# Linear attention and a two-layer Mish network: the hand-written order replaced by a list scheduler, both layers by seven products, attention by whole chunks

## The chip, the cores and the metric

The kernel runs on one core of a Trainium2 chip. The time is the device time of one execution in microseconds, taken as the median of several runs. A core has five engines that run side by side, each working through its own queue in order: TensorE (PE, matrix products), VectorE (DVE), ScalarE (ACT), GpSimd (POOL) and SyncE (SP, which issues transfers). They wait for one another by semaphores.

## The reference

The inputs are q, k, v of shape (4, 8, 768, 64) in fp32: 4 batches, 8 heads, 768 positions, 64 channels; `lam`, one decay for each head; w_in (512 x 2048) and w_out (2048 x 512).

```
for each block b of positions:
    intra = (qb kb^T * Dmask) vb                  # Dmask[i,j] = lam^(i-j) for i >= j, else 0
    inter = (qb * lam_pow) kv_state               # what earlier blocks left
    out[b] = intra + inter
    kv_state = lam_block * kv_state + (kb * rev_pow)^T vb
x = out, heads side by side                       # 3072 tokens x 512
h = x @ w_in
y = (h * tanh(softplus(h))) @ w_out               # Mish between the layers; 3072 x 512, fp32
```

## The kernel before

Both kernels take chunks of 128 positions. A **group** is one chunk of each of the four batches, 512 tokens; there are six groups, n = 0 to 5. For a group the attention makes `xt` (channels on the partitions, 4 x 512, fp16), the first layer makes h transposed in pieces of 128 x 512, Mish on ACT writes them to `hsg` in fp16, and the second layer multiplies `hsg` with `wout`.

**Attention** is done by half chunks, four heads each (`att_a`, `att_s`, `att_o`). From group 2 on, DVE scales q (`qT`, line 318) and copies k into `kz` (line 322), a tile in which the other head's 64 channels are zero, so that scores (`pS`, line 358) are products over all 128 partitions. DVE masks the scores into `sb` (line 362). `pO` (lines 375 and 379) adds up state and chunk; ACT copies it into `xt` (line 382). `pv` (line 283) is the new part of the state, which DVE adds (`raw`, line 298) and POOL multiplies with the decay (`w`, line 299). q and k arrive in fp16: POOL's queue casts them on the way. POOL scales k (`ktil`, line 259), and transfers that transpose, issued by SP, turn both (`qraw`, `kraw`, line 268); groups 0 and 1 are turned by PE.

**The first layer** is plain: 16 pieces of four products with 512 columns (`ph`, line 420). **The second layer** is plain in group 0 (`po`, line 442). From group 1 on it is done by seven products in place of eight (Strassen's way in Winograd's form; `fast_unit`, line 525): tokens, inner dimension and columns are halved, sums of quarters of `hsg` (`gsum`, line 498) and of `wout` (`tsum`, line 479) are made on DVE, and the seven products of 16 matmuls with 256 columns are gathered in `x`, `y`, `z`. ACT and DVE bring them out (`p1`, `p7`, `u3`, `osum`), POOL makes one difference (line 578).

**The order** is written out by hand. Each group has a list of `units`, the first layer's 16 pieces and then the second layer's 14; attention pieces of the next group are dealt out between them by `room`. An engine's queue is what this order leaves for it, and PSUM tiles have fixed uses by tag. The last group's last product lies in three PSUM tiles, `fin`, so that the last store is small.

**Loads** of q, k, v (but the first q and k) and of both weights go through POOL's queue, in the order chunks 0 to 3, `win` in six pieces, `wout` in four, chunk 4 and on. At most eight of its transfers are open: one waits until the eighth before it has landed.

Of the kernel before, what the change touches and what calls it, by code (L numbers as in the profile page):

```python
# [7 lines left out]
F32 = mybir.dt.float32  # L8
# [5 lines left out]
def bc(ap, axis, n):  # L14
    shape = list(ap.shape)
    shape.insert(axis, n)
    return ap.unsqueeze(axis).broadcast_to(shape)


@with_exitstack  # L20
def kernel(
# [19 lines left out]
    GT = B * C  # L41
    MID = C // 2 - 1
    NVB = 8
    NKB = 4
    NT = 2
# [3 lines left out]
    loads = ctx.enter_context(tc.tile_pool(name="loads", bufs=NVB))  # L49
    work = ctx.enter_context(tc.tile_pool(name="work", bufs=2))  # L50
    ps = ctx.enter_context(tc.tile_pool(name="ps", bufs=1, space=bass.MemoryType.PSUM))


    kn = [None] * (NG * B)
    qn = [None] * (NG * B)

    vz = [const.tile([128, H, 2 * D], F16, name=f"vz{i}") for i in range(NVB)]

    def chunk_rows(t, i):
        n, b = divmod(i, B)  # L60
        return t[b, :, n * C : (n + 1) * C, :].rearrange("h p c -> p h c")

    def load_k(i):
        if i == 0:
            kn[i] = const.tile([128, H, D], F32, name="kn0")
            nc.sync.dma_start(out=kn[i], in_=chunk_rows(k, i))
            return
        kn[i] = loads.tile([128, H, D], F16, name="kn", tag="kn")
        nc.gpsimd.dma_start(out=kn[i], in_=chunk_rows(k, i))  # L69

    def load_q(i):
        if i == 0:
            qn[i] = const.tile([128, H, D], F32, name="qn0")
            nc.scalar.dma_start(out=qn[i], in_=chunk_rows(q, i))
            return
        qn[i] = loads.tile([128, H, D], F16, name="qn", tag="qn")
        nc.gpsimd.dma_start(out=qn[i], in_=chunk_rows(q, i))  # L77

    def load_v(i):
        nc.gpsimd.dma_start(out=vz[i % NVB][:, :, 0:D], in_=chunk_rows(v, i))  # L80

    WS = 4

    cuts = (0, 128, 256, DF // WS)
    win0 = [const.tile([128, NKC, b_ - a_], F16, name=f"win0{a_}") for a_, b_ in zip(cuts, cuts[1:])]
    win = [None] + [const.tile([128, NKC, DF // WS], F16, name=f"win{s}") for s in range(1, WS)]
    wout = [const.tile([128, NKI // WS, DMO], F16, name=f"wout{s}") for s in range(WS)]

    def load_win(s):
        w = DF // WS  # L90
        if s == 0:
# [661 lines left out]
```

## Time and profile before

| | |
|---|---|
| runs | 219.47, 221.75, 222.33 us; median 221.75 |
| the profiled execution | span 217.4 us, from the first instruction to the last; the page has no other time of it |
| around the span | 4.35 us from the span to the median |
| busy in the span | PE 204.8, DVE 146.1, POOL 116.6, ACT 101.3 us |
| granted TensorE clock | 1.000 over the whole span |
| first product on the second piece of `win` | 21.13 us |
| last product | 214.06 us |

A row of the profile's groups names the line, the engine, the operation, out<-in, how often, the busy time and the mean of one in ns. A mean is the time from start to end of one instruction; two in a row on an engine overlap, so they follow each other at less than that. The chain of waits goes back from the last instruction, at each step to what released it.

### The profile page before, as it was taken

The numbers are of one execution on the slowest core, as the hardware profiler recorded it, in microseconds if no ns is written. First come the engines' busy times: TensorE is split into PE (matmuls) and PEld (weight loads), VectorE is DVE, ScalarE is ACT, GpSimd is POOL, SyncE is SP. The second block draws the span as 40 slices with busy tenths as digits, with TensorE's granted clock in tenths as the row PEclk, the third lists the DMA queues.
The fourth block names the chain that finished last, engine by engine and source line by source line (L and its number), as shares of the span: only waits on it lengthen the run. The fifth ranks groups of instructions, "written<-read, shape, count | busy, mean of one in ns | idle before, by whom it ended". The sixth has DMA issues, their size and how long they took to land.

```text
span 217.4 us, 4272 instructions
## 1 busy us (share of the span) xinstructions
PE 204.8 (94%) x1672; PEld 136.6 (63%) x1672; DVE 146.1 (67%) x309; ACT 101.3 (47%) x190; POOL 116.6 (54%) x139
## 2 busy tenths in 40 slices
PE   7899999999999799999979999979999999999993
PEld 2465544576545587745669845669845699644893
DVE  6667561877669999339999419999439987213433
ACT  5465566567665231166522176623166632266410
POOL 7996334998988768808757908757700002000020
PEclk9999999999999999999999999999999999999999
DMA  9999999999999999975999965999985201300014
GB/s 133 141 158 198 203 203 175 175 152 125 150 149 104 100 75 121 163 152 70 104 71 113 142 160 74 119 75 71 151 168 100 48 3 48 130 18 0 0 59 137
DMA packets 103766, 24.66 MB, mean 113 GB/s; under 512 B 93890, under 2 KB 103234, under 8 KB 103746
## 3 DMA queue, kind: packets, MB, share of 16 engines
q0 software_dynamic: 78080, 13.37, 80.3%
q1 hardware_dynamic: 22688, 8.39, 17.8%
q10 hardware_dynamic: 2978, 2.62, 4.0%
q8 instruction: 13, 0.21, 0.4%
q14 instruction: 7, 0.06, 0.1%
HBM read 27.26 MB, written 6.29 MB: 154 GB/s over the span
## 4 chain that ended last, share of the span: by engine, by line
PE 63%; DVE 20%; POOL 5%; issue 4%; DMA 4%; ACT 1%; ACTq 0%; POOLq 0%; DVEq 0%
PE ph L420 26%; PE z L525 10%; PE po L442 6%; PE y L525 6%; PE x L525 5%; DVE qT L318 5%; DVE kz L322 4%; DVE sb L362 4%; DVE gsum L498 4%; DMA win<-in_moe_w_in_dram 4%; PE pO L379 3%; DVE raw L298 3%; PE pS L358 2%; PE fin L525 2%; POOL vz L80 2%
## 5 line engine op out<-in xcount | busy, mean ns | idle before, releaser
L420 PE MATMUL ph<-xt,win 128*128 128x512 f16 (+2 forms) x404 | 89.6, 368 | 0.5 <-ACT hsg L434 0.2
L434 ACT ACTIVATE hsg<-ph 128x512 f16<-128x512 f32 x96 | 57.0, 597 | 45.6 <-PE ph L420 45.5
L420 PEld LDWEIGHTS <-win 128*128 128x128 f16 x404 | 37.0, 98 | 35.1 <-issue 0.6
L299 POOL TENSOR_TENSOR w<-raw,lbm 128x256 f16<-128x256 f32 x32 | 25.2, 791 | 29.0 <-DVE raw L298 28.9
L578 POOL TENSOR_TENSOR u<-u,p 128x512 f32<-128x512 f32 x5 | 6.5, 1293 | 52.0 <-DVE u L576 52.0
L525 PEld LDWEIGHTS <-gsum 128*128 128x128 f16 x336 | 30.8, 98 | 3.5 <-issue 0.5
L362 DVE TENSOR_TENSOR sb<-pS,maskT 128x512 f16<-128x512 f32 x40 | 27.2, 683 | 2.0 <-PE pS L358 1.9
L382 ACT ACTIVATE xt<-pO 128x256 f16<-128x256 f32 x40 | 15.2, 382 | 27.4 <-PE pO L379 27.2
L318 DVE TENSOR_TENSOR qT<-qraw,lq 128x256 f16<-128x256 f16 x32 | 19.1, 598 | 10.3 <-DMA qraw<-qn 10.3
L525 PEld LDWEIGHTS <-hsg 128*128 128x128 f16 x240 | 22.7, 98 | 2.5
L69 POOL DMA_DIRECT2D kn<-in_k_dram x23 | 21.4, 932 | 4.5 <-DMA win<-in_moe_w_in_dram 1.7
L80 POOL DMA_DIRECT2D vz<-in_v_dram x24 | 21.7, 906 | 3.3 <-DMA wout<-in_moe_w_out_dram 1.7
L77 POOL DMA_DIRECT2D qn<-in_q_dram x23 | 20.7, 898 | 5.1 <-DMA wout<-in_moe_w_out_dram 3.3
L498 DVE TENSOR_TENSOR gsum<-hsg 128x1024 f16<-128x1024 f16 x20 | 14.5, 725 | 12.9 <-ACT hsg L434 12.9
L322 DVE COPY kz<-kraw 64x256 f16<-64x256 f16 x64 | 19.9, 311 | 1.9 <-DMA kraw<-ktil 0.9
L379 PE MATMUL pO<-sb,vz 128*128 128x128 f16 x160 | 17.3, 219 | 3.6 <-DVE sb L362 3.2
L525 PE MATMUL z<-tsum,gsum 128*128 128x256 f16 x160 | 20.4, 272 | 0.2
L525 PE MATMUL x<-wout,hsg 128*128 128x256 f16 x160 | 20.1, 273 | 0.0
L358 PE MATMUL pS<-qT,kz 128*128 128x128 f16 x160 | 16.6, 220 | 1.8 <-DVE kz L322 1.6
L358 PEld LDWEIGHTS <-kz 128*128 128x128 f16 x160 | 11.8, 98 | 7.8 <-DVE kz L322 3.0
L298 DVE TENSOR_TENSOR raw<-pv,w 128x256 f32<-128x256 f32 x32 | 13.5, 422 | 4.1 <-PE pv L283 3.4
L379 PEld LDWEIGHTS <-vz 128*128 128x128 f16 x160 | 12.6, 98 | 5.7 <-issue 4.9
(89 smaller groups left out, 242.8 us busy)
## 6 DMA issues: line engine op xcount, KB each, us to landing
out_dram<-osum SPq DMA_DIRECT2D x14, 256.0 KB, 3.2
vz<-in_v_dram POOLq DMA_DIRECT2D x24, 128.0 KB, 4.7
kn<-in_k_dram POOLq DMA_DIRECT2D x23, 128.0 KB, 4.4
qn<-in_q_dram POOLq DMA_DIRECT2D x23, 128.0 KB, 4.6
wout<-in_moe_w_out_dram POOLq DMA_DIRECT2D x4, 512.0 KB, 16.5
win<-in_moe_w_in_dram POOLq DMA_DIRECT2D x3, 512.0 KB, 10.1
out_dram<-osum ACTq DMA_DIRECT2D x5, 256.0 KB, 4.0
out_dram<-osb ACTq DMA_DIRECT2D x4, 256.0 KB, 5.5
```

The costliest lines, as they stand in the source:

```text
L69: nc.gpsimd.dma_start(out=kn[i], in_=chunk_rows(k, i))
L80: nc.gpsimd.dma_start(out=vz[i % NVB][:, :, 0:D], in_=chunk_rows(v, i))
L299: nc.gpsimd.tensor_tensor(out=w_new, in0=raw, in1=lb, op=ALU.mult)
L318: nc.vector.tensor_tensor(out=s.qT, in0=qraw[i][:, 2 * hf : 2 * hf + 2, :], in1=lqh, op=ALU.mult)
L322: nc.vector.tensor_copy(s.kz[rs, :, hp, :], kraw[i][rs, 2 * hf : 2 * hf + 2, :])
L358: nc.tensor.matmul(psS[:, 2 * p + hp, :], s.kz[:, p, hp, :], s.qT[:, p, :], start=True, stop=True,)
L362: nc.vector.tensor_tensor(out=s.sb, in0=psS, in1=bc(maskT, 1, 4), op=ALU.mult)
L379: nc.tensor.matmul(psO[:, p, :], vf[:, o : o + 128], s.sb[:, 2 * p + hp, :], start=False, stop=(hp == 1))
L420: nc.tensor.matmul(ph_t[ni][:, lo:hi], win0[min(ni, 2)][:, kc, max(ni - 2, 0) * 128 : max(ni - 2, 0) * 128 + 128] if ni < w else win[ni // ...
L434: nc.scalar.activation(hsg[n][:, ni, :], ph_t.pop(ni), AF.Mish)
L498: nc.vector.tensor_tensor(out=gsum[n, i][:, ks, :], in0=a, in1=b, op=op)
L525: nc.tensor.matmul(t, lhs(kk, b), rhs(kk, c, c + w), start=(fresh and kk == 0 and (alone or i == 0)), stop=(kk == HK - 1), skip_group_chec ...
```

## The change

The kernel is rewritten. The parts that matter:

- **Order.** `Plan.op` records every operation with its engine, an estimate of its duration, a rank, and what it reads and writes. `Plan.run` takes, step by step, the operation that can start first (among those within `SLACK` of it the one of lowest rank), picks its engine and its buffer (eight PSUM banks shared by everything, with a least number kept for each use), and the instructions are issued in the order of the starts that it reckons. The chip's engines still wait by semaphores alone.
- **First layer** of groups 1 to 5 by seven products of four matmuls with 256 columns for each quarter `s` of the inner dimension (`first_layer`). Sums that were made outside PSUM in the second layer are made here by copying one PSUM bank into another, in which the next product is then accumulated: three copies on ACT or DVE and two additions on DVE for each quarter. Sums of `xt` and of `win` are made on DVE.
- **Second layer** of all groups by seven products, group 0 too; a 256 KB store at the end of each of its four results, the last one too.
- **Attention** by whole chunks: scores are products over 64 partitions, the two heads of a pair on the two halves of the array, into two banks; no `kz`. POOL scales both q and k (in groups 0 and 1 DVE does most of it). k, q of groups 1 to 5 are loaded in fp32 by SP; group 1 is turned by PE, later ones by transfers as before.
- **Loads.** `win` in four pieces. A small ACT copy that reads `win[2]` stands ahead of group 1's k and q, a small POOL copy that reads the fourth of them ahead of `wout`.
- `lq` is a decay for each position and head, made once; two table loads on ACT go.
- Empty products (`zero`) fill PE's idle time up to the 45th microsecond that `Plan.run` reckons.

The diff, cut to its core (the tile allocations, the launch and the set-up of decays are left out; lines of the old kernel are those on attention, first layer and order that are named above):

```diff
-            nc.vector.tensor_tensor(
-                out=s.qT, in0=qraw[i][:, 2 * hf : 2 * hf + 2, :], in1=lqh, op=ALU.mult)
-            for hp in range(2):
-                rs = slice(64 * hp, 64 * hp + 64)
-                nc.vector.tensor_copy(s.kz[rs, :, hp, :], kraw[i][rs, 2 * hf : 2 * hf + 2, :])
...
-        psS = ps.tile([128, 4, C], F32, name="pS", tag=("pS", "pk")[s.seq % 2 if s.n >= NT else 0])
-        for p in range(2):
-            for hp in range(2):
-                nc.tensor.matmul(
-                    psS[:, 2 * p + hp, :], s.kz[:, p, hp, :], s.qT[:, p, :], start=True, stop=True,
-                )
...
-        if hsg[n] is None:
-            hsg[n] = work.tile([128, NKI, GT], F16, name="hsg", tag="hsg", bufs=2)
-        if ni in ph_t:
-            mm1_part(n, ni, GT - C, GT)
-        else:
-            mm1_part(n, ni, 0, GT)
-        nc.scalar.activation(hsg[n][:, ni, :], ph_t.pop(ni), AF.Mish)
...
-    for n in range(NG):
-        units = [(mm1_unit, (n, ni)) for ni in range(NKI)]
-
-        if n == 0:
-            units += [(mm2_unit, (n, b2 + b, part)) for b2 in range(0, B, 2) for part in range(WS)
-                      for b in range(2)]
-        else:
-            units += [(fast_unit, (n, step, blk)) for step in range(7) for blk in range(2)]
...
+TAIL = {PE: 0.20, ACT: 0.15, DVE: 0.14, POOL: 0.12, SP: 0.0}
+SLACK = {PE: 0.12, ACT: 0.12, DVE: 0.12, POOL: 0.2, SP: 0.2}
...
+        while ready:
+            best = {}
+            for o in ready:
+                at = max([o.after] + [d.start for d in o.behind])
...
+                    for e, took in o.ways.items():
+                        if o.svc is not None and len(asked.get(e, ())) >= 8:
+                            at = max(at, asked[e][-8])
+                        t = max([at, free[e]] + [d.end if d.eng == e == PE else d.seen for d in o.deps])
+                        best.setdefault(e, []).append((t, o, took))
...
+            e, t0 = min(((e, min(c[0] for c in cs)) for e, cs in best.items()), key=lambda x: x[1])
+            t, o, took = min((c for c in best[e] if c[0] <= t0 + SLACK[e]), key=lambda c: (c[1].rank, c[0]))
+            other = [(c[0] + c[2], x) for x, cs in best.items() for c in cs if c[1] is o and x != e]
+            if other and min(other)[0] < t + took:
+                e = min(other)[1]
+                t, o, took = next(c for c in best[e] if c[1] is o)
...
+    banks = Pool([psum.tile([128, 512], F32, name=f"bank{i}") for i in range(8)],
+                 {"l1": 4, "l2": 1, "at": 2})
+    full = Pool(tiles("full", 13, [128, 512], F32), {"es": 2, "raw": 1, "l2": 8})
+    given = Pool(tiles("given", 8, [128, 512], F32))
+    half = Pool(tiles("half", 11, [128, 512], F16), {"kt": 2, "qt": 1})
+    turns = Pool(tiles("turn", 8, [128, 512], F16))
...
+            if (n, b) == (0, 0):
+                qe, chain = (SP if x == "k" else ACT), None
+            else:
+                qe, chain = (POOL, "sw") if n < 1 else (SP, "hw")
+            op({qe: 0.87 if qe == POOL else 0.42}, lambda e, buf=buf, src=src: ENG[e].dma_start(
+                out=by_head(buf.t), in_=rows(src, n, b)), rank, writes=[buf], svc=0.87, after=after,
+               chain=chain)
...
+    def scaled(n, b, src, by, name, rank, ways):
+        t = Buf(half, "kt" if name == "lk" else "qt")
+        op(ways, lambda e: ENG[e].tensor_tensor(
+            out=by_head(t.t), in0=by_head(src.t), in1=bc(by, 2, D), op=ALU.mult), rank,
+           reads=[src, name], writes=[t], chain=name)
+        return t
...
+    def turned(src, rank):
+        t = Buf(turns)
+        op({SP: 1.24}, lambda e: nc.sync.dma_start_transpose(out=by_pair(t.t), in_=src.t), rank,
+           reads=[src], writes=[t], svc=0.6, chain="turn")
+        return t
...
+            qT = turn(qt, rank - 2)
+        pS = [Buf(banks, "at") for _ in range(2)]
+
+        def scores(e):
+            for j in range(JP):
+                for t in range(2):
+                    rs = slice(64 * t, 64 * t + 64)
+                    nc.tensor.matmul(by_pair(pS[t].t)[:, j, :], by_pair(kT.t)[rs, j, :], by_pair(qT.t)[rs, j, :],
+                                     start=(j == 0), stop=(j == JP - 1), skip_group_check=True)
...
+            op({POOL: 1.25}, lambda e: nc.gpsimd.tensor_tensor(
+                out=wst[b], in0=by_pair(raw.t), in1=lbm, op=ALU.mult), late,
+               reads=[raw, "lbm"], writes=[("state", b)])
...
+    def first_layer(n, s, xs, rank):
+        kh, k0 = s // 2, 4 * (s % 2)
+        if s % 2 == 0:
+            gq[n, kh] = Buf(gblk)
+        A, Bb, Cc, E = (Buf(banks, "l1"), Buf(banks, "l1", seeded=True), Buf(banks, "l1", seeded=True),
+                        Buf(banks, "l1"))
+        es = Buf(full, "es")
...
+        def mish(src, r, f2, key):
+            op({ACT: 0.49}, lambda e: nc.scalar.activation(
+                gq[n, kh].t[:, r, k0 + 2 * f2 : k0 + 2 * f2 + 2, :], two(src.t), AF.Mish), rank + key,
+               reads=[src, "table"], writes=[(gq[n, kh], r, s % 2, f2)])
+
+        prod(A, w(0, 0), x(0, 0), True, lo + [("win", s)], 0)
+        op(cp(512), lambda e: copy(e, Bb.t, A.t), rank, reads=[A], writes=[Bb])
+        prod(E, w(0, 1), xsum(0), True, [xs[0], ("ws1", s)], 0.1)
+        prod(A, w(1, 0), x(1, 0), False, lo + [("win", s)], 0.3)
+        prod(Bb, ws(0), xsum(1), False, [xs[1], ("ws2", s)], 0.2)
+        op(cp(512), lambda e: copy(e, es.t, E.t), rank + 0.2, reads=[E], writes=[es])
+        opened["l1"] = op(cp(512), lambda e: copy(e, Cc.t, Bb.t), rank + 0.1, reads=[Bb], writes=[Cc])
+        op({DVE: 0.60}, lambda e: nc.vector.tensor_tensor(out=Bb.t, in0=Bb.t, in1=es.t, op=ALU.add), rank + 0.3,
+           reads=[es], writes=[Bb])
+        prod(Cc, ws(1), xsum(2), False, [xs[2], ("ws3", s)], 0.2)
+        prod(Bb, ws(2), x(1, 1), False, hi + [("ws4", s)], 0.5)
+        op({DVE: 0.60}, lambda e: nc.vector.tensor_tensor(out=es.t, in0=Cc.t, in1=es.t, op=ALU.add), rank + 0.3,
+           reads=[Cc], writes=[es])
+        prod(Cc, w(1, 1), xsum(3), False, [xs[3], ("win", s)], 0.4)
+        mish(A, 0, 0, 0.8)
+        mish(Bb, 1, 0, 0.8)
+        mish(es, 1, 1, 0.8)
+        mish(Cc, 0, 1, 0.8)
...
+        def store(r, c, t, rk):
+            op({SP: 0.42}, lambda e: nc.sync.dma_start(
+                out=out_v[n * C : (n + 1) * C, 2 * r : 2 * r + 2, c * HN : (c + 1) * HN], in_=two(t.t)),
+               rank + rk, reads=[t], svc=0.8)
...
+    k_first = buffers(1, 0)[0]
+    op({ACT: 0.2}, lambda e: nc.scalar.activation(k_first.t[:, 0:1], win[2][:, 0, 0:1], AF.Copy), -595,
+       reads=[("win", 2)], writes=[k_first])
+    for b in range(B):
+        load(1, b, "kq", -590 + b)
+    k_late = buffers(1, 1)[1]
+    op({POOL: 0.1}, lambda e: nc.gpsimd.tensor_copy(wout[0][:, 0, 0:1], k_late.t[:, 0:1]), -581,
+       reads=[k_late], writes=[("wout", 0)], chain="sw")
+    for s in (0, 2, 1, 3):
+        load_wout(s, -580 + s)
...
+    for s in range(WS):
+        first_plain(0, s, 10 * s)
...
+    order = plan.run()
+    rest = {a: (gap, s) for a, gap, s in plan.idle(banks, 45.0, 0.4)}
+    for o in order:
+        o.fn(o.eng)
+        if o in rest:
+            for _ in range(int((rest[o][0] - 0.15) / 0.219)):
+                nc.tensor.matmul(rest[o][1].tile, zero[:, 0:128], zero, start=False, stop=True,
+                                 skip_group_check=True)
...
```

Three places in which the order is new. First **POOL's queue after the first chunks' loads** (each row issues a load). Before:

```order
L96 DMA win_81<-in_moe_w_in_dram 128x4x512
L96 DMA win_82<-in_moe_w_in_dram 128x4x512
L103 DMA wout_83<-in_moe_w_out_dram 128x4x512
L103 DMA wout_84<-in_moe_w_out_dram 128x4x512
L103 DMA wout_85<-in_moe_w_out_dram 128x4x512
L103 DMA wout_86<-in_moe_w_out_dram 128x4x512
L140 IOTA ei 128x128
L69 DMA kn<-in_k_dram 128x8x64
L77 DMA qn<-in_q_dram 128x8x64
```

and now, with `given_89` the q of chunk 5:

```order
L351 DMA win_161<-in_moe_w_in_dram 128x4x512
L351 DMA win_162<-in_moe_w_in_dram 128x4x512
L411 DMA vz_136<-in_v_dram 128x8x64
L411 DMA vz_137<-in_v_dram 128x8x64
L411 DMA vz_138<-in_v_dram 128x8x64
L411 DMA vz_139<-in_v_dram 128x8x64
L735 CAST wout_167<-given_89 128x1
L356 DMA wout_167<-in_moe_w_out_dram 128x4x512
L356 DMA wout_169<-in_moe_w_out_dram 128x4x512
```

`wout` has moved from right behind `win` to behind group 1's v and the fourth of group 1's k and q.

Second **DVE's queue at the second layer of group 0**: the sums of `wout` (`wos`, and one half of `wout` in place) and of the group's hidden values (`g`, `gsum`). Now:

```order
L364 TENSOR_TENSOR g_115<-g_115,g_116 128x1024
L364 TENSOR_TENSOR wos_172<-wout_170,wout_168 128x1024
L364 TENSOR_TENSOR wos_171<-wout_169,wout_167 128x1024
L364 TENSOR_TENSOR wout_168<-wout_168 128x4x256
L364 TENSOR_TENSOR wos_171<-wout_169,wos_171 128x1024
L364 TENSOR_TENSOR wos_172<-wout_170,wout_168 128x1024
L364 TENSOR_TENSOR g_115<-g_115,g_116 128x1024
L364 TENSOR_TENSOR wos_172<-wout_170,wos_172 128x1024
L364 TENSOR_TENSOR gsum_120<-g_115 128x1024 x2
L364 TENSOR_TENSOR gsum_121<-g_116,gsum_120 128x1024 x2
```

From the second row on all of them are behind the last piece of `wout` (`wout_170`). Before, the same eight sums (`tsum`) stood among the units of groups 0 and 1 and were first needed in group 1.

Third **ACT's queue in the first layer of a later group** (`hsg` before, `g` now: Mish; `bank` PSUM; `full` SBUF in fp32). Before:

```order
L434 ACTIVATE hsg<-ph 128x512 x11
L382 ACTIVATE xt<-pO 128x2x128
L434 ACTIVATE hsg<-ph 128x512 x3
L382 ACTIVATE xt<-pO 128x2x128
L434 ACTIVATE hsg<-ph 128x512 x2
```

and now:

```order
L252 ACTIVATE bank_70<-bank_65 128x512
L252 ACTIVATE full_75<-bank_67 128x512
L252 ACTIVATE full_76<-bank_66 128x512
L581 ACTIVATE g_115<-bank_65 128x512
L252 ACTIVATE bank_69<-bank_64 128x512
L252 ACTIVATE full_78<-bank_63 128x512
L581 ACTIVATE g_115<-full_75 128x512
L252 ACTIVATE bank_67<-bank_69 128x512
L581 ACTIVATE g_115<-bank_70 128x512
L581 ACTIVATE g_115<-bank_68 128x512
L581 ACTIVATE g_115<-bank_64 128x512
L252 ACTIVATE bank_63<-bank_66 128x512
```

Copies from bank to bank, for which PE's next product waits, now stand between the Mish instructions.

1041 lines of the change are left out of this document (501 added, 540 removed).

## The prediction

> **What bounds the kernel now.** I read the page's busy times first, then the busy time by stage, then the chain of waits, and last the rows of the groups and of POOL's queue that price single steps.
>
> ```profile
> PE 204.8 (94%) x1672; PEld 136.6 (63%) x1672; DVE 146.1 (67%) x309; ACT 101.3 (47%) x190; POOL 116.6 (54%) x139
> PE 63%; DVE 20%; POOL 5%; issue 4%; DMA 4%; ACT 1%; ACTq 0%; POOLq 0%; DVEq 0%
> ```
>
> PE is busy 94% of the span and it holds 63% of the chain; DVE holds 20%. Where DVE's 20% lies, the stages tell (start and end, length, then busy time of each engine). I cut them at the beginning of each group's first layer, as the chain shows it; the first cut is the product that waits for the second piece of `win`, the last one the end of PE.
>
> ```profile
> core 0: us, PE busy (x) PEld busy (x) DVE busy (x) ACT busy (x) POOL busy (x), PEclk, DMA share, GB/s
> 0.00:21.10 21.10, 17.80 (x144) 9.98 (x144) 14.29 (x38) 11.42 (x20) 18.08 (x28) 1.00 1.58 156
> 21.10:57.00 35.90, 35.42 (x276) 20.68 (x277) 23.34 (x52) 22.71 (x46) 24.73 (x30) 1.00 1.49 172
> 57.00:90.65 33.65, 31.01 (x261) 21.68 (x261) 26.41 (x52) 13.22 (x26) 27.98 (x32) 1.00 1.49 115
> 90.65:124.05 33.40, 31.98 (x274) 22.65 (x272) 25.52 (x52) 14.21 (x27) 22.20 (x26) 1.00 1.05 112
> 124.05:157.50 33.45, 32.02 (x273) 22.65 (x272) 25.54 (x52) 14.21 (x27) 21.10 (x24) 1.00 1.04 111
> 157.50:188.00 30.50, 30.50 (x257) 21.67 (x256) 21.49 (x48) 14.17 (x27) 1.27 (x1) 1.00 0.36 76
> 188.00:214.10 26.10, 26.04 (x192) 17.32 (x190) 9.27 (x17) 11.35 (x19) 1.27 (x1) 1.00 0.12 41
> ```
>
> Groups 4 and 5 (157.5 to 214.1) are PE without a gap, and the granted clock is 1.00 in every stage. In groups 1 to 3 DVE is busy 25.5 of 33.4 us, and the chain runs over it. To see what PE alone needs I take the pace of its products from pieces of the chain, and the pace of products over 64 partitions from the timeline.
>
> ```profile
> 187.97 13.81 PE ph L420 x64
> 201.78 1.75 PE x L525 x16
> 114.07 0.22 PE pS L358 x4
> 113.91 0.39 PE L358 MATMUL pS<-qT,kz 128*128 128x128 f16 x4
> 15.45 0.40 PE L230 MATMUL pS<-pqT,pkT 64*128 64x128 f16 x8
> ```
>
> A product of 512 columns follows the last after 13.81/64 = 0.216 us, one of 256 after 0.109, one of 128 after 0.055. In the last two rows eight products over 64 partitions take from start to end what four over 128 take: they run in pairs, so eight cost 0.22.
>
> So PE needs in a middle group before: first layer 13.8; second layer 7 x 16 x 0.109 = 12.2; attention 4 chunks x (8 scores + 12 outputs + 4 states) x 0.055 = 5.3; together 31.3. Groups 2 and 3 take 33.4: 2.1 are waits, DVE's.
>
> **The change part by part.**
>
> *PE's work.* First layer by seven products: 7 x 4 x 4 = 112 matmuls at 0.109 = 12.2 for 13.8, 1.6 less in each of groups 1 to 5. Scores in pairs: 4 x 0.22 = 0.9 less in each of groups 1 to 4's attention work. A middle group needs 12.2 + 12.2 + 4.4 = 28.9; group 4, without states, 28.0; group 5 24.5.
>
> *The hand-offs of the first layer.* They are new on the path: for each quarter a copy of a bank before the next product can begin, twice in a row, and an addition. In groups and timeline before, the nearest rows:
>
> ```profile
> L434 ACT ACTIVATE hsg<-ph 128x512 f16<-128x512 f32 x96 | 57.0, 597 | 45.6 <-PE ph L420 45.5
> 56.36 1.08 ACT L434 ACTIVATE hsg<-ph 128x512 f16<-128x512 f32 x2 [0.49 <-PE ph L420]
> L362 DVE TENSOR_TENSOR sb<-pS,maskT 128x512 f16<-128x512 f32 x40 | 27.2, 683 | 2.0 <-PE pS L358 1.9
> 13.24 1.29 DVE L234 TENSOR_TENSOR sb<-pS,dm 128x512 f16<-128x512 f32 x2 [0.49 <-PE pS L230]
> ```
>
> ACT takes 0.597 for one, but two follow each other after 1.08 - 0.597 = 0.49; DVE after 1.29 - 0.683 = 0.60. By the order ACT has 32 such instructions in a middle group (16 Mish, 9 copies in the first layer, 3 in the second, 4 of `xt`): 15.7 us of 29. DVE has 39: 35 at 0.60 and 4 sums of `xt` of half that size, 22.2 us. Neither is the bound over a group. Inside the first layer it is close: 25 on ACT make 12.3 us against PE's 12.2, though PE's last product of the layer waits for only 18 of them, 8.8 us. That a copy writes PSUM is in no row. It reads 512 columns of PSUM like these rows, which excludes less than ACT's 0.49; above I bound it by DVE's 0.683 with no overlap, and take 0.49, its nearest form. A hand-off is longer than that: four products at a pace of 0.055 take 0.39 from start to end (row above), so a result is out 0.17 after PE could go on; with ACT's whole 0.597 and two semaphores it is 0.84. A quarter's chain is five products of 0.44 and four hand-offs, 5.6 us; the order has two quarters in flight, which fits into 12.2 with a little to spare. I allow 1.2 us of waits in groups 1 to 3, 1.0 in groups 4 and 5, where there were 2.1 and none; bounds 0 and 3.5.
>
> *Transfers of q and k, scaling on POOL.* Per group POOL has 8 scalings, 4 states and one difference:
>
> ```profile
> L578 POOL TENSOR_TENSOR u<-u,p 128x512 f32<-128x512 f32 x5 | 6.5, 1293 | 52.0 <-DVE u L576 52.0
> L80 POOL DMA_DIRECT2D vz<-in_v_dram x24 | 21.7, 906 | 3.3 <-DMA wout<-in_moe_w_out_dram 1.7
> 91.93 1.22 SPq L268 DMA_TRANSPOSE qraw<-qn  x1
> 0.74 0.45 SPq L66 DMA_DIRECT2D kn<-in_k_dram  x1
> qraw<-qn SPq DMA_TRANSPOSE x16, 3.4
> ```
>
> 13 x 1.29 + 4 x 0.91 = 20.4 of 29 us. SP has 8 transposing issues of 1.22, 8 loads and 4 stores of 0.45, 15 us. Both run a group ahead, under the 12.2 us of a second layer; where that cover is gone, the first late transpose costs its landing, 3.4 us. I put them at nothing.
>
> *The start, and group 0.* POOL's queue shows when the weights land: each load waits until the eighth before it has landed.
>
> ```profile
> 18.72 0.92 POOL L69 DMA_DIRECT2D kn<-in_k_dram  x1 [0.42 <-issue]
> 21.39 0.87 POOL L77 DMA_DIRECT2D qn<-in_q_dram  x1 [1.75 <-DMA win<-in_moe_w_in_dram]
> 23.87 0.87 POOL L80 DMA_DIRECT2D vz<-in_v_dram  x1 [1.61 <-DMA win<-in_moe_w_in_dram]
> 26.42 0.88 POOL L69 DMA_DIRECT2D kn<-in_k_dram  x1 [1.67 <-DMA win<-in_moe_w_in_dram]
> ...
> 36.60 0.87 POOL L77 DMA_DIRECT2D qn<-in_q_dram  x1 [1.68 <-DMA wout<-in_moe_w_out_dram]
> ```
>
> The first quarter of `win` is in by 18.7, all of it by 26.4 and `wout` by 36.6, a piece each 2.55 us; q, k, v follow at POOL's 0.87. Now 4 loads of v and 8 of fp32 k, q come between: 26.4 + 12 x 0.87 + 4 x 2.55 = 47.0 for the last of `wout`. For SP's fp32 loads the trace has one of the kind, 3.0 us from issue to landing:
>
> ```profile
> kn<-in_k_dram SPq DMA_DIRECT2D x1, 256.0 KB, 3.0
> L498 DVE TENSOR_TENSOR gsum<-hsg 128x1024 f16<-128x1024 f16 x20 | 14.5, 725 | 12.9 <-ACT hsg L434 12.9
> ```
>
> Bounds for one of many are 0.64, a quarter of a weight piece (1 MB of fp32 in 2.55), and 1.5, half of the 3.0: 44.3 to 52 for `wout`. I keep 0.87, between them, the pace at which POOL fed such loads. PE by then has done its other work: first layer from about 18.7, 13.8 + turning 1.8 + states 0.9 + attention 4.4 + two early products 0.9 brings it to 40.5, and it idles for `wout`. Behind the last piece DVE makes nine sums before the product that needs the last of them, 9 x 0.69 (a little under the row's mean of 0.725, since they follow each other) = 6.2, and half of the second layer, 6.1, is still to come: group 0 ends at 59.3, say 59.0, for 57.0 before. So the gain of a seven-product layer there (1.6) and of the pairs is lost in the wait for `wout`: +2.0 (bounds -0.5 and +8).
>
> *The end.* The last result is one addition and one 256 KB store, where there were small pieces:
>
> ```profile
> 214.08 0.29 DVE osum L562
> out_dram<-osum SPq DMA_DIRECT2D x14, 256.0 KB, 3.2
> out_dram<-osum SPq DMA_DIRECT2D x2, 64.0 KB, 1.7
> ```
>
> Addition 0.68 for 0.29, landing up to 3.2 for 1.7, shorter in an empty queue: 4.6 from PE's end to the span's for 3.3, +1.3 (bounds 0.5 and 1.9).
>
> *Sum* against the profiled execution, span 217.4: start +2.0; group 1 28.9 - 0.9 (done early) + 1.2 = 29.2 for 33.65, -4.4; groups 2 and 3 30.1 for 33.4, -6.6 together; group 4 29.0 for 30.5, -1.5; group 5 25.5 for 26.1, -0.6; end +1.3. In all -9.8: a span of 207.6. The runs' median, 221.75, lies 4.35 above the span; I take that for what lies around it: **212.0 us**.
>
> **A rule that speaks against it.** DVE can be held by POOL:
>
> ```profile
> 70.48 2.05 DVE L318 TENSOR_TENSOR qT<-qraw,lq 128x256 f16<-128x256 f16 x1
> 70.47 0.77 POOL L299 TENSOR_TENSOR w<-raw,lbm 128x256 f16<-128x256 f32 x1
> 71.16 1.08 POOL L259 TENSOR_TENSOR ktil<-kn,lk 128x512 f16<-128x512 f16 x1
> L318 DVE TENSOR_TENSOR qT<-qraw,lq 128x256 f16<-128x256 f16 x32 | 19.1, 598 | 10.3 <-DMA qraw<-qn 10.3
> ```
>
> An instruction of 0.41 took 2.05, to the end of POOL's two; the mean is 0.60, 0.19 too much. The Trainium skill, page "SBUF — State Buffer", section "Who interferes with whom", says that a DVE instruction with two SBUF inputs and a GpSimd one that reads SBUF exclude each other for a whole instruction; the trace agrees, by these rows. Now 12 sums of a group's 39 DVE instructions have two inputs in SBUF, and POOL computes 13 x 1.29 = 16.8 us a group. At the mean's 0.19 that is 2.3 us, inside DVE's 29 - 22.2 = 6.8 of slack; at the worst row's 1.64 each it is 19.7.
>
> **The rivals.** (1) *POOL's lock on DVE*: with 7 of the 12 sums held as in the worst row, 11.5 - 6.8 = 4.7 us are on the path in four groups, 212 + 19 = 231, slower; it decides from 5.6 of 12 on (where 2.4 a group eat the 9.8). For it: POOL computes more than before. Against: the mean of 32 rows. (2) *First-layer hand-offs queue behind Mish* on ACT, 0.75 us each: a quarter's chain is 8.6, two at a time make 17.2 a layer, 3.8 over what I allow, in five groups: 231, slower. For it: ACT is as long as PE in that stretch. Against: 18 of 25 are enough, and PE has other work at its edges. (3) *wout comes at 52 or later*, or SP's transposes lag behind its stores: group 0 ends 6 us on, 218, no change. For it: all of these loads share one path. Against: its upper bound is needed. (4) *The paper does not hold on PE*, the pairs run one by one: +0.9 in each of four groups, 215.6, still faster. (5) *No waits at all*: 212 - 5.6 = 206.4.
>
> **How the numbers follow.** About 2%, 4.4 us, can be told from no change: faster is below 217.3, slower above 226.2. Forecast 0.60; (5) 0.06; (4) 0.05; (3) with half sizes of (1) and (2) 0.14; (1) 0.06; (2) 0.09. Faster 0.71, same 0.14, slower 0.15. The forecast's own range is 207 to 217; to hold 8 in 10 with the middle cases it goes from 205.5 to 222.
>
> **What would show it.** Right: second layer of group 0 ending at 57 to 62, its products or their sums waiting for `wout`; groups 1 to 3 at 29 to 31; PE pieces of first-layer products at 0.44 for four, eight scores in 0.4 from start to end; SP's transposes landed before they are needed. Wrong: a wait of PE for ACT or DVE of over 3 us in each group's first layer; DVE's sums at means over 1.2 us; a throttled clock; `wout` after 52.

## The result, and the profile after

The changed kernel takes 235.25 us (median of 4 runs, 232.45 to 236.78) against 220.88 for the kernel before on the same chip: a ratio of 1.0575, with an interval of 1.0466 to 1.0683. It is slower by 14 us; 212.0 had been forecast, and the range ended at 222. The profiled execution has a span of 232.4 us (its own time 234.12). Medians, here and below, are of all runs of a kernel; ratios leave out executions more than 1.5% above the kernel's fastest.

From the page after, PE's busy time and the granted clock in 40 slices; then the busy time by stage, cut as before at the beginning of each group's first layer (the first row ends at group 0's first layer, the last is the end behind PE).

```profile
PE 206.8 (89%) x1949; PEld 162.3 (70%) x1949; DVE 175.6 (76%) x283; ACT 109.0 (47%) x203; POOL 101.0 (43%) x101
PEclk9999999769799999997999999999999999999999
0.00:19.20 19.20, 17.11 (x137) 9.57 (x138) 16.00 (x43) 9.62 (x17) 16.04 (x25) 1.00 1.57 154
19.20:75.80 56.60, 43.22 (x336) 27.84 (x334) 43.05 (x66) 17.76 (x31) 26.38 (x26) 0.91 1.24 178
75.80:109.95 34.15, 31.25 (x315) 26.02 (x313) 27.30 (x38) 16.28 (x31) 22.20 (x20) 0.95 1.09 178
109.95:143.45 33.50, 30.58 (x324) 26.13 (x322) 27.49 (x39) 16.86 (x32) 23.07 (x22) 1.00 1.23 179
143.45:173.95 30.50, 30.46 (x323) 26.04 (x321) 24.96 (x39) 16.86 (x32) 10.76 (x9) 1.00 0.30 70
173.95:203.20 29.25, 29.25 (x306) 25.09 (x305) 20.95 (x35) 16.85 (x32) 1.27 (x1) 1.00 0.11 37
203.20:228.20 25.00, 24.97 (x225) 21.64 (x222) 15.11 (x23) 14.71 (x28) 1.27 (x1) 1.00 0.13 44
228.20:232.40 4.20, 0.00 (x0) 0.00 (x0) 0.69 (x1) 0.00 (x0) 0.00 (x0) 0.87 0.34 116
```

| stage | forecast | measured |
|---|---|---|
| group 0 ends | 59.0 | 75.8 |
| group 1 | 29.2 | 34.15 |
| group 2 | 30.1 | 33.5 |
| group 3 | 30.1 | 30.5 |
| group 4 | 29.0 | 29.25 |
| group 5 | 25.5 | 25.0 |
| end | 4.6 | 4.2 |

The last four stages came as forecast. All of the error is in group 0 (+16.8), group 1 (+5.0) and group 2 (+3.4): the stages in which POOL does most of its scaling of later groups' q and k (26, 22 and 23 us of POOL there, 11 and then 1.3 behind). PE's waits name two places:

```profile
PE bank L664 <- DVE full L695: 5.6, 3, 2.6
PE bank L443 <- POOL half L426: 5.1, 1, 5.1
PE bank L664 <- DVE wos L364: 4.4, 1, 4.4
```

**The first place, POOL and DVE.** From the timeline of group 0's second layer, DVE's sums of `wout` and POOL's scalings side by side (start, length, engine and line):

```profile
57.16 2.62 DVE L364 TENSOR_TENSOR g<-g,g 128x1024 f16<-128x1024 f16 x1
59.70 2.97 DVE L364 TENSOR_TENSOR wos<-wout,wout 128x1024 f16<-128x1024 f16 x2
62.60 1.52 DVE L364 TENSOR_TENSOR wout<-wout 128x1024 f16<-128x1024 f16 x1
64.05 1.53 DVE L364 TENSOR_TENSOR wos<-wout,wos 128x1024 f16<-128x1024 f16 x1
65.49 1.53 DVE L364 TENSOR_TENSOR wos<-wout,wout 128x1024 f16<-128x1024 f16 x1
66.94 0.68 DVE L364 TENSOR_TENSOR g<-g,g 128x1024 f16<-128x1024 f16 x1
...
43.78 1.04 POOL L426 TENSOR_TENSOR half<-given,lq 128x512 f16<-128x512 f32 x1 [6.60 <-DMA given<-in_q_dram]
57.60 1.06 POOL L426 TENSOR_TENSOR half<-given,lk 128x512 f16<-128x512 f32 x1
59.54 1.13 POOL L426 TENSOR_TENSOR half<-given,lq 128x512 f16<-128x512 f32 x1
60.65 1.48 POOL L426 TENSOR_TENSOR half<-given,lk 128x512 f16<-128x512 f32 x1
62.09 1.48 POOL L426 TENSOR_TENSOR half<-given,lq 128x512 f16<-128x512 f32 x1
63.54 1.48 POOL L426 TENSOR_TENSOR half<-given,lk 128x512 f16<-128x512 f32 x1
64.99 1.48 POOL L426 TENSOR_TENSOR half<-given,lq 128x512 f16<-128x512 f32 x1
```

They start in turns: DVE at 62.60, 64.05 and 65.49, POOL at 62.09, 63.54 and 64.99, each every 1.45 us. Alone a sum takes 0.68 (66.94, as soon as POOL has stopped) and a scaling 1.04 (43.78). So both are longer, and each step is nearly one instruction of each, one after the other (1.45, where the two alone take 1.72). PE waits 4.36 us for one of these sums, then 1.42 and 0.59. In group 1 the same pair stands, with the sums of `xt` (`xsum`) behind it, ahead of the additions that hand over the second layer's results (L695), and in group 2 at 131 to 138:

```profile
96.09 2.82 DVE L364 TENSOR_TENSOR gsum<-g 128x1024 f16<-128x1024 f16 x2
98.83 2.97 DVE L364 TENSOR_TENSOR gsum<-g,gsum 128x1024 f16<-128x1024 f16 x2
98.32 1.49 POOL L426 TENSOR_TENSOR half<-given,lq 128x512 f16<-128x512 f32 x1
```

**The second place, chunk 7's q.** PE waits 5.12 us, to 44.88, for its scaling (43.78 above), and POOL waits for its transfer. POOL had issued `wout` nine us before, and the transfers' own table has 5 to 6 us to landing for q and k where the trace before showed 3.0:

```profile
33.68 0.19 POOL L735 CAST wout<-given 128x1 f16<-128x1 f32 x1 [16.84 <-DMA given<-in_q_dram]
34.20 2.98 POOL L356 DMA_DIRECT2D wout<-in_moe_w_out_dram  x4 [0.33 <-POOL wout L735]
given<-in_k_dram SPq DMA_DIRECT2D x21, 256.0 KB, 5.1
given<-in_q_dram SPq DMA_DIRECT2D x20, 256.0 KB, 5.8
```

In the trace's packets, SP's queue moves 4,156 from 30 to 35 us, but 786 from 40 to 45, where POOL's moves 791, nearly all of `wout`: about one of each in turn, and those of `wout` are four times as large.

**The clock.** In and behind PE's longer waits the granted clock falls; for the wait that ends at 44.88 it is 0.50 from 43.5 to 50.4 (windows cut at the waits; the clock is the third number from the end):

```profile
40.00:44.80 4.80, 0.00 (x0) 0.00 (x0) 0.49 (x1) 0.59 (x2) 1.02 (x2) 0.87 1.21 195
44.80:48.00 3.20, 3.12 (x27) 2.65 (x29) 1.62 (x3) 0.94 (x2) 3.08 (x4) 0.50 1.22 196
105.00:108.00 3.00, 3.00 (x17) 2.07 (x15) 0.50 (x1) 0.00 (x0) 3.00 (x4) 0.50 0.60 124
139.80:143.00 3.20, 3.20 (x30) 2.86 (x30) 1.38 (x2) 0.00 (x0) 3.17 (x3) 1.00 0.40 126
```

### The profile page after: what moved, and what is told of

It is laid out like the page before. It is cut to its first block, busy times and chain, and to the rows that moved or that the text cites. A ratio compares the mean times of both kernels' runs of the same rounds, so it can differ in the third digit from the quotient of the medians.

```text
span 232.4 us, 4925 instructions
## 1 busy us (share of the span) xinstructions
PE 206.8 (89%) x1949; PEld 162.3 (70%) x1949; DVE 175.6 (76%) x283; ACT 109.0 (47%) x203; POOL 101.0 (43%) x101
## 4 chain that ended last, share of the span: by engine, by line
PE 46%; DVE 5%; DMA 2%; issue 0%; DVEq 0%
PE bank L562 22%; PE bank L664 20%; DVE gsum L364 2%; DMA turn<-half 2%; PE bank L496 2%; PE bank L472 1%; PE bank L492 1%; DVE xsum L364 1%; DVE full L695 1%; DVE full L523 1%; DVE g L364 1%; PE bank L511 0%; DVE bank L254 0%; DVE sb L482 0%; DVEq L695 0%
## 5 line engine op out<-in xcount | busy, mean ns | idle before, releaser
L664 PEld LDWEIGHTS <-g 128*128 128x128 f16 x384 | 37.7, 100 | 13.5 <-issue 6.3
L664 PE MATMUL bank<-wout,g 128*128 128x256 f16 x288 | 35.5, 273 | 1.4 <-DVE g L364 1.4
L581 ACT ACTIVATE g<-bank 128x512 f16<-128x512 f32 x60 | 32.6, 607 | 1.6 <-PE bank L562 1.3
L695 DVE TENSOR_TENSOR full<-bank,full 128x512 f32<-128x512 f32 x24 | 16.6, 690 | 22.0 <-PE bank L664 21.7
L664 PE MATMUL bank<-wos,gsum 128*128 128x256 f16 x192 | 25.2, 282 | 5.3 <-DVE wos L364 4.4
L562 PEld LDWEIGHTS <-wis 128*128 128x128 f16 x240 | 23.0, 97 | 5.6 <-issue 2.0
L526 POOL TENSOR_TENSOR state<-full,lbm 128x512 f16<-128x512 f32 x16 | 22.7, 1431 | 8.4 <-DVE full L523 8.3
L482 DVE TENSOR_TENSOR sb<-bank,mask 128x512 f16<-128x512 f32 x40 | 26.2, 684 | 0.2 <-PE bank L472 0.2
L562 PE MATMUL bank<-xsum,wis 128*128 128x256 f16 x160 | 24.0, 272 | 0.3 <-DVE bank L254 0.3
L562 PE MATMUL bank<-xt,win 128*128 128x256 f16 x160 | 23.0, 276 | 0.0
L562 PE MATMUL bank<-xsum,win 128*128 128x256 f16 x160 | 22.5, 273 | 0.0
L252 ACT ACTIVATE xt<-bank 128x512 f16<-128x512 f32 x24 | 14.4, 602 | 13.1 <-PE bank L496 12.1
L592 DVE TENSOR_TENSOR bank<-bank,full 128x512 f32<-128x512 f32 x20 | 13.9, 695 | 8.7 <-ACT bank L252 8.7
```

The costliest lines, as they stand in the source:

```text
L252: nc.scalar.activation(out_, in_, AF.Copy)
L482: op(TT, lambda e, t=t: nc.vector.tensor_tensor(out=by_pair(sb[t].t), in0=by_pair(pS[t].t), in1=bc(mask, 1, JP), op=ALU.mult), rank, reads ...
L526: op({POOL: 1.25}, lambda e: nc.gpsimd.tensor_tensor(out=wst[b], in0=by_pair(raw.t), in1=lbm, op=ALU.mult), late, reads=[raw, "lbm"], writ ...
L562: nc.tensor.matmul(two(bank.t)[:, f, :], lhs(kc, f), rhs(kc), start=(fresh and f == 0 and kc == 0), stop=(f == 1 and kc == 1), skip_group_ ...
L581: op({ACT: 0.49}, lambda e: nc.scalar.activation(gq[n, kh].t[:, r, k0 + 2 * f2 : k0 + 2 * f2 + 2, :], two(src.t), AF.Mish), rank + key, re ...
L592: op({DVE: 0.60}, lambda e: nc.vector.tensor_tensor(out=Bb.t, in0=Bb.t, in1=es.t, op=ALU.add), rank + 0.3, reads=[es], writes=[Bb])
```

## The experiments

The order of PE, DVE and ACT is the changed kernel's in all of them, but for the empty products of the fourth and for the eighth. "A chunk's q" counts chunks over the groups: chunk 5 is the second of group 1, chunk 7 its last.

**1. POOL's scaling without its reads.** In place of a scaling, POOL copies one column and fills the rest twice with a constant, so q and k of groups 2 to 5 and chunk 7's q are not scaled.

```diff
-ENG[e].tensor_tensor(out=by_head(t.t), in0=by_head(src.t), in1=bc(by, 2, D), op=ALU.mult)
+nc.gpsimd.tensor_copy(t.t[:, 0:1], src.t[:, 0:1])
+for _ in range(2):
+    nc.gpsimd.memset(t.t[:, 1:512], 0.01)
```

> In this run POOL does not scale q and k of groups 1 (one of eight) to 5: it reads one column and fills the tile with a constant by two memsets, so the values are not the reference's; the order on all engines is that of the changed kernel. Theory A (POOL instructions that read SBUF hold DVE's sums with two inputs in SBUF, and the other way round): DVE's sums of wout fall from 1.5 to about 0.7 us each, the 4.4 us wait of PE for them goes, group 0 ends at 66 to 69 instead of 75.8, groups 1 and 2 take 30 to 31 instead of 34.2 and 33.5, the span is 216 to 220 instead of 232.4. Theory B (DVE's sums are slowed by the transfers' traffic in SBUF, or DVE simply has too much to do there): the sums stay at 1.2 to 1.5 us and the span within 3 us of 232.

Measured: 221.44 (8 runs), ratio 1.0023 [0.9972, 1.0073]. The sums are short again, but for those that meet the state products that POOL still does (its rows: form and count, then least, median and longest ns):

```profile
L364 DVE TENSOR_TENSOR wos<-wout,wout x4: 677/680/1754, 52.4 to 59.7; 128x1024 f16<-128x1024 f16 x4
```

Group 0 ends at 69.1, and groups 1 and 2 take 31.8 and 30.8. The transfers are as they were, and POOL is as busy as before in these places (1.10 us for the two fills that replace 1.04 of scaling), so it is POOL's reading that makes DVE's sums long, not the traffic.

**2. wout released by chunk 7's q.**

```diff
-wout[0][:, 0, 0:1], k_late.t[:, 0:1]
+wout[0][:, 0, 0:1], buffers(1, 3)[1].t[:, 0:1]
```

> One operand is changed: the small POOL copy that stands ahead of wout's loads reads the last q of group 1 (chunk 7) instead of the fourth of its k and q. Nothing else moves. Theory C (chunk 7's q is late, at 43.8, because 4 MB of wout are let in ahead of it): it lands at 37 to 40, PE's wait of 5.1 us for its scaling goes or falls under 1.5, TensorE's clock stays at 1.00 there, wout lands 3 to 6 later, and the span is 4 to 9 us shorter unless wout is then waited for. Theory D (it is late because SP's queue goes on with group 2's loads, or because of its own slow issue): it lands at 42 or later, and the span grows by 0 to 5.

Measured: 231.93, ratio 1.0508 [1.0367, 1.0648], about 3 less than the changed kernel, whose runs spread over more than that. POOL's timeline:

```profile
39.09 0.19 POOL L735 CAST wout<-given 128x1 f16<-128x1 f32 x1 [21.88 <-DMA given<-in_q_dram]
39.61 2.98 POOL L356 DMA_DIRECT2D wout<-in_moe_w_out_dram  x4 [0.33 <-POOL wout L735]
42.58 1.08 POOL L426 TENSOR_TENSOR half<-given,lq 128x512 f16<-128x512 f32 x1
```

The copy went off at 39.09, so chunk 7's q had landed by then, where POOL waited for it to 43.78 before: `wout` had been in its way. But POOL now issues `wout` ahead of the scaling, 3 us, and PE's wait fell only from 5.1 to 4.2. Each place is from one execution: run 4, which leaves the transfers alone, has this scaling at 40.89, so part of the 4.7 us can be scatter.

**3. Group 2's loads held until wout has landed.** SP first moves two bytes out of the last quarter of `wout`.

```diff
+if o.fn is hold.get("fn"):
+    nc.sync.dma_start(out=mark[0:1, :], in_=wout[3][0:1, 0, 0:1])
 o.fn(o.eng)
```

> One transfer of two bytes that reads the last piece of wout is put into SP's queue ahead of group 2's loads of k and q, so that these wait until wout is in. Theory D (group 2's fp32 loads, of which SP has issued several by 43 us, delay chunk 7's q and wout): chunk 7's q lands at 38 to 41, PE's wait falls to 0 to 2 us, wout is in 3 to 6 us earlier, and the span is 3 to 8 shorter unless group 2's scaling becomes late. Theory C (wout alone is in its way): chunk 7's q lands at 42.5 to 44 as before, and the span is the same or longer by the later loads of group 2.

Measured: 233.73, two runs, no interval. Chunk 7's q was scaled no earlier, at 46.37. Group 2's loads stand behind it in SP's queue and are not what delays it. Alone this edit brought nothing that can be told.

**4. PE kept busy while it waits.** 24 empty products ahead of the one that waits for chunk 7's q.

```diff
+for _ in range(24):
+    nc.tensor.matmul(spare.tile, zero[:, 0:128], zero, start=False, stop=True, skip_group_check=True)
```

> 24 empty products (5.2 us) are put into PE's queue ahead of the transposes that wait for chunk 7's q; nothing else moves. If it is the idle time that halves the clock afterwards: the wait ends at the same place, 44.5 to 45.5, the granted clock from 44.8 to 50 is 1.00 instead of 0.50 to 0.70, and PE reaches the second layer of group 0 at 51.5 to 52.5 instead of 54.6; the span is 0 to 2.5 us shorter, since DVE's sums behind it are held by POOL all the same. If the clock falls for another reason (the work itself): 0.5 to 0.7 stays.

Measured: 233.27, ratio 1.0568 [1.0479, 1.0658].

```profile
40.00:56.00 16.00, 14.51 (x133) 9.46 (x132) 11.08 (x16) 4.47 (x8) 11.53 (x11) 1.00 1.36 184
60.00:64.00 4.00, 4.00 (x26) 3.02 (x24) 4.00 (x5) 0.68 (x2) 2.77 (x3) 0.64 1.21 180
```

The clock stays at 1.00 behind that wait, and X, the first product of group 0's second layer, begins at 52.5 in place of 54.6 us. The wait was not the same, though that had been expected: chunk 7's q was scaled at 40.89, and it was the empty products that held PE to 44.48, in place of 44.88. So some 1.6 of the 2.1 us are the clock's. The clock falls again behind the next wait, for `wos`. In the time of the runs these 2 us are within what the two kernels' runs spread.

**5. POOL's scaling of groups 2 to 5 behind the last xsum of the group before.** Everything is computed.

```diff
+gate = last_sum.get(n - 1)
+def go(e):
+    if gate and b == 0:
+        nc.gpsimd.tensor_copy(t.t[:, 0:1], gate.t[:, 0, 0:1])
+    ENG[e].tensor_tensor(out=by_head(t.t), in0=by_head(src.t), in1=bc(by, 2, D), op=ALU.mult)
...
-reads=[src, name]
+reads=[src, name] + ([gate] if gate else [])
```

> Every product and sum is kept, and the order on TensorE, VectorE and ScalarE is the changed kernel's, row for row. Only POOL's scaling of q and k of groups 2 to 5 now waits for the last of the four xsums of the group before (a one-column copy of it), so that it falls under a first layer, where VectorE's operations have a PSUM bank among their operands, and no longer beside the sums of wout, g and xt. If POOL and VectorE block each other when both read and write SBUF alone (theory A): the wos and gsum sums fall from 1.5 to 0.68 us each, PE's waits of 4.4 us for wos and of 2.6 us for L695 in groups 1 and 2 go, the scaling takes 1.04 us, and the time is 217 to 222 us, as it was without the scaling's reads. If the DMA traffic is what makes them long (B): the sums stay at 1.5 us and the time at 231 to 236. If the scaling is then too late for the attention that needs it: PE waits for turn in the first layers, and the time is 225 to 230.

Measured: 220.8 (10 runs, 215.92 to 223.0, the clock 0.975 to 1.00), ratio 0.9844 [0.978, 0.9909]. The profiled execution has a span of 217.6, 14.8 below the changed kernel's; PE still waits 3.4 us for chunk 7's q in it.

```profile
L433 POOL TENSOR_TENSOR half<-given,lq x17: 1042/1044/1045, 42.4 to 163.7; 128x512 f16<-128x512 f32 x17
L364 DVE TENSOR_TENSOR wos<-wout,wout x4: 676/677/1753, 51.7 to 59.0; 128x1024 f16<-128x1024 f16 x4
```

No scaling is longer than 1.045 us, though DVE works beside it: it now meets additions and copies with a PSUM bank among their operands. The stage ends give what it was worth: group 0 ends at 68.5 (-7.3), group 1 takes 29.6 (-4.6), group 2 30.5 (-3.0). X begins 1.2 us earlier than in the changed kernel (53.4), with chunk 7's q; the sums from 57.16 to 66.94 above take 3.6 us here for 9.8, which is 6.2 of the 7.3.

**6. The gate, and wout behind the scaling of chunk 7's q.**

```diff
-wout[0][:, 0, 0:1], k_late.t[:, 0:1]
+wout[0][:, 0, 0:1], q_last[0].t[:, 0:1]
```

> The kernel with the gate on POOL's scaling, and also the copy that releases wout reads the scaled q of chunk 7 in place of the given q of chunk 5, so the four wout loads are issued behind that scaling. If wout's packets and POOL's 3 us of issuing are what makes chunk 7's q late (C): it is scaled at about 40 us in place of 43.8, PE's wait of 5.1 us falls below 1.5, the clock stays at 1.00 from 40 to 56 us, and the time is 5 to 8 us below the kernel with the gate alone, 211 to 215 us. If wout is then too late for the second layer: the X product waits for the wout transfer, the gain is 0 to 3 us. If neither matters: no change, 217 to 222.

Measured: 222.35, ratio 1.0106 [1.0064, 1.0147]: the expected gain did not come.

```profile
39.11 1.04 POOL L433 TENSOR_TENSOR half<-given,lq 128x512 f16<-128x512 f32 x1 [22.25 <-PE bank L506]
55.03 2.72 PE L674 MATMUL bank<-wout,g 128*128 128x256 f16 x12 [6.18 <-DMA wout<-in_moe_w_out_dram]
```

The first half of theory C held (chunk 7's q is scaled at 39.1, PE's wait for it is 0.9), and the wait went to `wout`, which PE reached 6.2 us early. In these runs the late q and the late `wout` are one shortage: whichever is put first, the other is late.

**7. The gate, wout released by chunk 6's q, and group 2's loads held.** The gate of 5, the two bytes of 3, and `buffers(1, 2)[1]` in the copy of 2.

> The kernel with the gate on POOL's scaling, order of PE, VectorE, ScalarE and POOL row for row, with two edits to the transfers: the copy that releases wout reads the given q of chunk 6 in place of that of chunk 5, and SP's first load of group 2 waits until the last quarter of wout has landed (a transfer of two bytes that reads it), so that wout shares the DMA engines with fewer packets of q and k. If it is the sharing of the DMA engines that makes either chunk 7's q or wout late (C and D together): q of chunk 7 is scaled by 41.5, wout lands by 50, PE waits under 1.5 us for each, the clock stays at 1.00 and the time is 210.5 to 214 us. If chunk 7's q is late by itself: PE's wait of 3.4 us stays, the clock falls to 0.5 behind it, 217 to 222. If wout is late in turn: the X product waits 3 to 6 us for it, 215 to 220.

Measured: 216.4 (4 runs, 215.84 to 218.16), ratio to the kernel before 0.9844 [0.9768, 0.992]. It is below both kernels, and by 0.8 to 2.3% below the one before; the 210.5 to 214 expected were missed. The rows are cut up to 0.5 us behind each group's first product:

```profile
19.20:64.30 45.10, 39.89 (x339) 26.29 (x337) 36.84 (x67) 17.66 (x31) 20.77 (x24) 1.00 1.38 186
64.30:96.10 31.80, 29.65 (x315) 25.31 (x313) 24.73 (x39) 16.28 (x31) 19.43 (x20) 1.00 1.04 182
126.60:157.00 30.40, 30.36 (x322) 25.95 (x320) 24.87 (x40) 16.86 (x32) 15.42 (x16) 1.00 0.72 145
81.82 0.40 PE L481 MATMUL bank<-turn,turn 64*128 64x128 f16 x8 [2.08 <-DMA turn<-half]
```

Group 0 ends at 63.9, 4.6 earlier than in 5, and the clock is 1.00 up to the last product. The fastest runs of 5 and 7 are alike, though (215.92 and 215.84), and the profile of 5 is of one of its longer runs, so it isn't shown that the edits do more than keep the long runs away. PE's wait for chunk 7's q is 1.9, where I had expected under 1.5, and a new wait of 2.1 for a transposed tile is in group 1.

**8. The same with plain first layers.** All groups go through `first_plain`, and POOL's scaling waits for a gsum.

```diff
-first_layer(n, s, xs, 100 * n + 10 * s)
+first_plain(n, s, 100 * n + 10 * s)
```

> The kernel of the run before, but all six groups take the first layer by plain products (eight in place of seven, 512 columns each), so the sums of win and of xt and the first layer's additions are left out; POOL's scaling then waits for the last gsum of the group two before. Every output is kept. If seven products are worth on PE what the prediction took from the rows (1.6 us a group and more, PE being what bounds groups 1 to 5): 5 x 1.6 = 8 us slower than the run before, 218 to 222. If the copies and additions between the banks give back what the products save: within 3 us of it.

Measured: 219.61 (10 runs, 218.82 to 220.1), 3.2 above 7.

```profile
125.40:156.90 31.50, 31.50 (x274) 21.40 (x273) 16.39 (x24) 13.73 (x23) 17.34 (x17) 1.00 1.11 153
```

Groups 2 to 5 take 31.5, 31.5, 30.5 and 26.0 for 30.5, 30.4, 29.3 and 25.0: the seven products bring 1.0 to 1.2 a group, not 1.6. Group 1 has none of the wait that 7 has, so 7 gives 2 us back there.

**9. Group 2's loads held less long.** `mark` reads `wout[1]`, the third quarter to be issued, in place of `wout[3]`.

> The kernel with the gate on POOL's scaling, wout released by chunk 6's q, and group 2's loads held; now they are held only until the third of the four quarters of wout has landed, not the last. If PE's wait of 2.1 us for a transposed tile in group 1 comes from group 2's loads starting too late (their first issue at 52.0): they start about 3 us earlier, that wait is gone, wout's last quarter lands at most 1 us later, and the time is 1 to 3 us less, 213 to 215.5. If that wait is POOL's (its scalings start when the xsums are done, whatever the loads do): no change, 215.5 to 217.5.

Measured: 218.94 (10 runs, 217.45 to 220.29), ratio 0.993 [0.9892, 0.9968], 2.5 above 7. The wait for the transposed tile fell from 2.08 to 0.84, as expected, but X begins at 50.9 for 49.1 and group 0 ends at 66.0 for 63.9; in the profiled execution the first layer of group 0 also began 0.9 late, which this edit doesn't touch. A miss in the time; the mechanism was there. Whether the 2 us of group 0 are the edit's is open.

**10. The transfers' edits of 7 without the gate.**

> The changed kernel with the two edits to the transfers alone (wout released by chunk 6's q, SP's loads of group 2 held until wout has landed), without the gate on POOL's scaling. If the blocking of POOL and VectorE is most of the loss: its sums of g and xt in groups 1 and 2 are 1.5 us and more again, PE waits 2.6 us for L695 in each, and the time is 7 to 12 us above the kernel with the gate and the same transfers (216.4), 224 to 229; less than in the changed kernel in group 0, since held loads also bring POOL's scaling of group 2 behind the sums of wout. If transfers were most of it: 216 to 220.

Measured: 229.02 (4 runs), ratio 1.0366 [1.0288, 1.0443], 12.6 above 7, a little more than the 7 to 12 expected.

```profile
56.17 5.29 POOL L430 TENSOR_TENSOR half<-given,lk 128x512 f16<-128x512 f32 x1 [3.50 <-DMA given<-in_k_dram]
57.07 1.28 DVE L364 TENSOR_TENSOR gsum<-g 128x1024 f16<-128x1024 f16 x2
92.20 3.20 DVE L364 TENSOR_TENSOR gsum<-g,gsum 128x1024 f16<-128x1024 f16 x2
93.37 1.49 POOL L430 TENSOR_TENSOR half<-given,lq 128x512 f16<-128x512 f32 x1
```

The held loads bring group 2's scaling behind the sums of `wout`. The first of them starts while DVE's sums run one behind the other; here it is POOL that is held, 5.29 us, and the sums stay at 0.68 (1.28 for two), so group 0 ends at 64.7. Later scalings then stand beside group 1's sums, and group 1 takes 39.4. So the blocking doesn't go away with the transfers, it moves.

Together, by the medians: from 235.25 the transfers' edits alone take 6.2 us and the gate a further 12.6; the other way round the gate alone takes 14.4 and the transfers' edits 4.4, the step that the fastest runs do not show.

## Why the prediction was wrong

**Rival (1), POOL's lock on DVE, is what happened;** I gave it 0.06. The step that failed is the price "At the mean's 0.19 that is 2.3 us, inside DVE's 29 - 22.2 = 6.8 of slack", and beside it "I put them at nothing" for POOL's scaling. Runs 1 and 5 show that the two engines do hold each other. The Trainium skill, page "SBUF — State Buffer", section "Who interferes with whom", which the prediction cited, was right in that. The mean of 32 rows in the kernel before was the wrong row to size it by: 22 of those 32 met no product of POOL at all (0.41 to 0.43 us each), and the three that were held longest took 1.83 to 2.05. What counted was which instructions stand side by side: in group 0 six sums in a row meet six scalings (57.16 to 66.94), the four gsums and the xsums behind them meet three scalings and two state products in group 1, two and two in group 2. The six sums took 9.8 us, and 3.6 in run 5; these 6.2 us are most of the 7.3 that the gate brought in group 0. Slack over a group is no cover either, when the sums stand right ahead of what PE waits for. The rival's own size, 19 us in four groups, was near the 12.6 to 14.8 that the gate brought; its place was not (three stages, half of it in group 0). In group 3 two gsums still took 2.84 us beside POOL's state products, and PE did not wait for them.

**The start.** "26.4 + 12 x 0.87 + 4 x 2.55 = 47.0" for the last of `wout` failed by the pace and by leaving the loads of group 2 out. From issue to landing of its four pieces (least, median, longest), in the changed kernel and in 7:

```profile
DMA to landing us min/median/max: 7.7/11.6/15.6
DMA to landing us min/median/max: 5.9/9.0/11.7
```

The last is issued at 36.4 and 39.1, so `wout` is in at 52.0 and 50.8, near the upper bound of 44.3 to 52. The first was issued at 34.2, ahead of the 36.8 in the sum; but the four then took 17.8 us to be in, not 4 x 2.55 = 10.2, and 13.9 in run 7, where group 2's loads are held. In the changed kernel it wasn't PE's first wait: X began at 54.6, after the wait for chunk 7's q and the slow clock behind it, which the prediction didn't have. With the scalings moved and the transfers eased (run 7), group 0 ends at 63.9 for 59.0: 3.8 of these 4.9 are `wout`'s landing. The rest lies ahead of the nine sums: the sum before them still meets one of POOL's state products (1.75 us from 49.74), the first of the nine begins at 52.02, and PE waits 1.3.

**The clock** was taken as 1.00. It was 0.91 in group 0 and 0.95 in group 1, behind waits that were not foreseen; a consequence, and by run 4 worth some 1.6 us for the first of them.

**What was right.** The hand-offs of the first layer cost nothing (rival 2): PE waits 0.3 us in it. Groups 3 to 5 came within 0.5 us. The middle group's parts were less right than their sum: PE is busy 30.46 of 30.5 without a gap, where 28.9 of work and 1.2 of waits had been reckoned. Counted from the start of one product to the start of the next, group 3's first layer takes 12.8 us for 12.2, its second 12.6 for 12.2, its scores 1.3 for 0.9: the paces were a little short, and waits that did not come made up for it, which was luck. The first layer's saving is 1.0 to 1.2 (run 8). The end took 4.2 for 4.6. The copy of a bank into a bank, reckoned at ACT's 0.597, took 0.601:

```profile
L252 ACT ACTIVATE bank<-bank 128x512 f32<-128x512 f32 x31 | 18.6, 601 | 39.9 <-PE bank L562 39.9
```

The 4.35 us around the span was too much: in the runs here 1.7 us lie between the span and its own time. So run 7, with most of the loss cured, is 7.5 us above the forecast in its span (215.1 for 207.6) and only 4.4 in its time: the forecast lost too little in the span and added too much around it.

## What to carry to other kernels

Price a blocking between two engines by the instructions that the order puts side by side, not by the mean of a kernel where they seldom met: where POOL's product of two tensors stands beside DVE's sum of two tensors in SBUF, reckon them one after the other, and look at which of the two PE waits for. Work that "lies beside" something is free only beside the right something: the same scalings cost nothing under the first layer, where DVE's operands include PSUM, and over 12 us beside the sums. A transfer that is moved to another queue still shares the DMA engines with all that is issued near it, and what gives way there is the small packets.

## What the runs showed of the hardware that I had not expected

- The blocking can lengthen both sides: DVE's sum from 0.68 to 1.5 and POOL's scaling from 1.04 to 1.48 us, a step each 1.45. It can also fall on one: in run 10 a scaling took 5.29 us while the sums beside it stayed at 0.68. What decides between the two was not tested.
- The clock after a wait isn't a plain function of its length: after 5.1 us it was 0.50; after 2.58 us, before 105, it was 0.50, and after 2.57 us, before 139.8, it was 1.00. In the changed kernel's trace the slow stretches last 3.41 us or twice that, and they begin at 43.54, 60.61 and 104.98, whole multiples of 3.41 apart. Cut into such steps, the wait before 105 lies in one of them (101.57 to 104.98), and the wait before 139.8 falls into two, 1.9 and 0.7 us. That the idle share of one step decides is a reading of these figures and was not tested.
- Two queues that are both full share by the packet, not by the byte: 786 of SP's (256 bytes) and 791 of POOL's (1 KB, `wout`) in the same 5 us.
